# Seven products in the first layer from the third chunk on, its squares on ScalarE, three pieces of MLP work kept back

## The chip, the cores and the metric

The kernel runs on one core of a Trainium2 chip. TensorE multiplies matrices into PSUM, VectorE (DVE in the profile), ScalarE (ACT) and GpSimd (POOL) do the elementwise work, and SyncE (SP) and GpSimd issue DMA transfers. Each engine works through its own instructions in the order in which they were written and waits on semaphores for the others. The metric is the device time of the whole program in microseconds; lower is better.

## What is computed

```python
# attention: q, k, v are (8, 8, 576, 64), float32
scores = (1.0 / np.sqrt(64)) * np.matmul(q, k.transpose(0, 1, 3, 2))
thresh = np.max(scores, axis=-1, keepdims=True) - tau
scores = np.where(scores >= thresh, scores, -1000000000.0)
scores = scores - np.max(scores, axis=-1, keepdims=True)
attn = np.exp(scores)
attn = attn / (np.sum(attn, axis=-1, keepdims=True) + 1e-09)
attn_out = np.matmul(attn, v)
# bridge: (B, H, S, D) -> x of (4608, 512)
x = attn_out.transpose(0, 2, 1, 3).reshape(4608, 512)
# MLP: w_in is (512, 2048), w_out is (2048, 512)
h = x @ w_in
r = np.maximum(h, 0.0)
g = r * r
out = g @ w_out
```

## The kernel before

**Steps of attention.** Two heads (a pair) are worked on together. A step `s` takes one block of 128 query rows of one pair: scores on TensorE (line 249), their maxima on VectorE (L271), exponentials on ScalarE (L284 to L287), threshold and row sum on VectorE (L299 to L302), division on GpSimd (L307 and L309). The weights are then turned, in the first 35 steps by TensorE (L341), from step 35 on (`first_dma`) by VectorE in blocks of 32 (L381) and by DMAs (L393, L398), and multiplied with v (`mix`, L443); the result is copied into the ring of tokens `xT` (L426 to L437). There are 148 steps. The program's last pass, at step 151 (`END`), holds all that is left.

**Chunks of the MLP.** The 4608 tokens make 18 chunks of 256. A chunk's MLP work is queued when its last token is there: chunk 0 at step 10, chunk 1 at step 21, chunks 2 and 3 at step 43, then two or three at a time at steps 61, 79, 97, 115, 133 and 151. Chunk 0 (`PLAIN = 1`) is computed plainly: 16 pieces of the first layer (`mlp_in`, L491) and 16 of the second (`mlp_out`, L663). All later chunks use the seven products of a 2 x 2 block scheme (Strassen's, in Winograd's form) in both layers: 14 `unit` pieces of the first layer (seven products, two halves, L595) and 14 halves of products of the second (`product`, L698). Each piece is a group of TensorE matmuls.

**What the seven products need.** In the first layer they need differences of tokens, T1 to T4 (L568), and sums of weights (`factor_sum`, L536), made per chunk on VectorE or GpSimd, and one difference, S3, that replaces a block of `w_in` in place (`in_place`, L514). A product lands in a PSUM bank; ScalarE copies it into g (L615, L620, L624) or VectorE adds it (L607), then comes Relu on ScalarE (L603) and the square on GpSimd (L604). In the second layer they need four differences of `w_out`, made once in 16 parts (`some_sums`, L651), and differences of g (`square_half`, L481 and L482, and L718, L722).

**Order.** The order on each engine is that of the Python code. The loop over steps writes the attention instructions and calls `fill` four times per step, which takes pieces from the queue `waiting` by a planned rate (`rate`): each piece counts 1.76 us, and the rate is the smallest of "work at hand by then, divided by steps until then" over the coming arrivals and the end. A piece is also gated by how many blocks of weights have been loaded and rounded; the pieces of chunk 1 and later ask for one more than there are, which `state["usable"]` grants from step 38 on. `ask` queues sums of VectorE, `some_later` issues them one at a time between other work, and `need` issues at once what a unit is about to read. What follows a piece (copies, adds, squares) is returned as a list and written one piece later (`after`).

**Before step 43.** From step 35 on, `early_work` gives VectorE two operations per step: the four in-place differences S3 (L514), then the weight sums of chunk 1's products "6" and "5". Chunk 1 keeps its own places for sums (`home`), since g is empty then.

Of the kernel before, what the change touches and what calls it, by code (L numbers as in the profile page):

```python
# [19 lines left out]
def kernel(  # L20
# [10 lines left out]
    nc = tc.nc  # L31
# [11 lines left out]
    TCH = 2 * P  # L43
    NCH = n_tokens // TCH
    HF, HD = NFT // 2, d_model // 2
    PLAIN = 1
    SCALE = 0.125
    assert (H % 2, D, REST, NBLK, d_model) == (0, 64, 64, 4, H * D)
    assert n_tokens == B * S and n_tokens % TCH == 0 and SCALE * SCALE * D == 1.0
# [434 lines left out]
    def mlp_in(j, x):  # L484

        f, at = FORDER[x], j * TCH % RING
        if x % 2 == 0:
            used["h"] = take("mm", (6, 7))
        h = used["h"].rearrange("p (f n) -> p f n", f=2)
        for c in range(NMC):  # L490
            nc.tensor.matmul(h[:, x % 2, :], w_in_sb[:, c, f * P:(f + 1) * P], xT[:, c, at:at + TCH],  # L491
                             start=(c == 0), stop=(c == NMC - 1))
        if x == NFT - 1:
            read_to["x"] = (j + 1) * TCH
        if x % 2 == 0:
            return []

        def square():
            to = g[:, f - 1:f + 1, :]
            nc.scalar.activation(out=to, in_=h, func=AF.Relu)  # L500
            nc.gpsimd.tensor_tensor(out=to, in0=to, in1=to, op=ALU.mult)
        return [square]

    def block_of(name, q, c):
# [5 lines left out]
    def in_place():  # L510

        def one(q, c):
            to = w_in_sb[:, c, DH + q * WP:DH + (q + 1) * WP]
            nc.vector.tensor_tensor(out=to, in0=w_in_sb[:, c, q * WP:(q + 1) * WP], in1=to, op=ALU.subtract)  # L514
        return [lambda q=q, c=c: one(q, c) for q in range(2) for c in range(2)]

    def halves_of(t, lo):
        return [t[:, lo + x:lo + x + 2, :].rearrange("p f n -> p (f n)") for x in (0, 2)]
# [2 lines left out]
    low, high = ([x[:, lo:lo + HF // 2, :].rearrange("p f n -> p (f n)") for x in gsum] for lo in (0, HF // 2))  # L521

    def home(j, p, q):

        if j == PLAIN and q == 0:
            return {"6": low, "5": high, "3": gb}[p]
# [32 lines left out]
    def some_later(count=1):  # L559

        for _ in range(min(count, len(later))):
            j, p, *rest = later.popleft()
            if p[0] != "T":
                factor_sum(j, p, *rest)
                continue
            x11, x12, x21, x22 = tokens(j)
            to, a, b = {"T1": (T1, x12, x11), "T2": (T2, x22, T1), "T3": (x12, x22, x12), "T4": (T4, x21, T2)}[p]
            nc.vector.tensor_tensor(out=to, in0=a, in1=b, op=ALU.subtract)  # L568

    def need(*what):  # L570
        for x in what:
            assert x in asked
            while x in later:
                some_later()

    def unit(j, p, q):

        if (p, q) == ("1", 0):
            ask((j, "T1"), (j, "T2"), (j, "T3"))
            if j == PLAIN:  # L580
                ask((j, "3", 0, 0), (j, "3", 0, 1))
        if j == PLAIN:
            some_sums(1)
        if p in "5674":
            need((j, {"5": "T1", "6": "T2", "7": "T3", "4": "T4"}[p]))
        if (p, q) in (("3", 0), ("6", 1), ("5", 1), ("3", 1)):
            need((j, p, q, 0), (j, p, q, 1))
        x11, T3, x21, x22 = tokens(j)
        part = {"1": x11, "2": x21, "3": x22, "5": T1, "6": T2, "7": T3, "4": T4}[p]
        if p in "125":  # L590
            used[p, q] = keep_bank((p, q))
        to = used[{"6": "1", "7": "1", "4": "1", "3": "5"}.get(p, p), q].rearrange("p (f n) -> p f n", f=4)
        for f in range(4):
            for c in range(2):
                nc.tensor.matmul(to[:, f, :], factor(j, p, q, c)[:, f * P:(f + 1) * P], part[:, c, :],  # L595
                                 start=(p in "125" and f == 0 and c == 0), stop=(p in "234" and f == 3 and c == 1),
                                 skip_group_check=True)
        if (p, q) == UNITS[1][0]:
            read_to["x"] = (j + 1) * TCH
        g11, g12, g21, g22 = (g[:, lo + 4 * q:lo + 4 * q + 4, h * P:(h + 1) * P] for lo in (0, HF) for h in range(2))  # L600

        def square(to, src=None):
            nc.scalar.activation(out=to, in_=to if src is None else src, func=AF.Relu)  # L603
            nc.gpsimd.tensor_tensor(out=to, in0=to, in1=to, op=ALU.mult)  # L604

        def add(x):
            nc.vector.tensor_tensor(out=x, in0=to, in1=x, op=ALU.add)  # L607
            return [lambda: square(x)]

        def then():  # L610
            more = []
            if p == "1":
                if q:
                    need((j, "3", 0, 0), (j, "3", 0, 1))
                nc.scalar.copy(g11, to)  # L615
                ask((j, "T4"))
            elif p == "2":
                more = add(g11)
            elif p == "6":
                nc.scalar.copy(g12, to)  # L620
                if q:
                    ask((j, "3", 1, 0), (j, "3", 1, 1))
            elif p == "5":
                nc.scalar.copy(g22, to)  # L624
                if not q:
                    if j == PLAIN:
                        ask(*((j, x, 1, c) for x in "6" for c in range(2)))
# [54 lines left out]
    def product(j, x, half):  # L682
# [23 lines left out]
        def then():  # L706
# [12 lines left out]
            elif p == "6":  # L719
                tt(out=p1s, in0=to, in1=p1s, op=add)  # L720
                nc.gpsimd.tensor_tensor(out=c12, in0=p5s, in1=p1s, op=add)
                halves(lambda f: tt(out=gsum[1][:, f, :], in0=g1[:, f, 0:P], in1=gsum[1][:, f, :], op=sub))  # L722
                for c in range(2):
                    factor_sum(j + 1, "6", 0, c, nc.gpsimd)
            elif p == "7":
# [30 lines left out]
    def by_dma(n):  # L756

        return n >= 3 * HP - 1
# [25 lines left out]
            j += 1  # L784
    PIECE_US = 1.76
    VALUES_US = 4.8
    waiting = deque()
    state = {"us": 0.0, "left": 0.0, "step": 0, "free": False, "rounded": 0, "usable": 0, "then": [], "last": []}

# [20 lines left out]
    def rate(s):  # L810


        if s < out_from:
            return PIECE_US * sum(x[2] == 0 for x in waiting) / (out_from - s)
        have = PIECE_US * len(waiting) - state["left"]
        best = 1e9
        at = s
        for e in sorted(chunk_at) + [END]:
            if e > s:
                have += sum(VALUES_US for x in range(at, e) if x in mixes and by_dma(mixes[x][0]))  # L820
                at = e
# [13 lines left out]
    def piece():  # L835
        _, fn, *what = waiting.popleft()
        state["left"] -= PIECE_US
        if fn is mlp_out or what[0] < PLAIN and what[1] == 0 or what == [PLAIN, "1", 0]:
            after()
        then = fn(*what)  # L840
        after()
# [29 lines left out]
    early_work = deque()  # L871

    def end_rounding(p):
        round_weights(p, 4)
# [54 lines left out]
    rounded_by = [0]  # L929
    for s in range(END + 1):  # L930
        state["step"] = s
        state["usable"] = rounded_by[-1] + (s > first_dma + 2)
        if s == 2:
            startup.close()
            bpsum = ctx.enter_context(tc.tile_pool(name="bpsum", bufs=1, space=bass.MemoryType.PSUM))
            bank.update((x, bpsum.tile([P, 512], FP32, tag=f"bank{x}", name=f"bank{x}")) for x in range(4, 8))
        rounded_by.append(state["rounded"])
        if s == first_dma:
            assert read_to["x"] == PLAIN * TCH
            work = in_place() + [lambda p=p, c=c: factor_sum(PLAIN, p, 0, c) for p in ("6", "5") for c in range(2)]  # L940
# [57 lines left out]
        if on:  # L998
# [78 lines left out]
```

## Time and profile before

| | |
|---|---|
| median of 3 runs | 1403.05 us (1402.34 to 1405.98) |
| the profiled execution | 1405.17 us, of which the span is 1403.4 us |
| mean granted TensorE clock | 0.984 |
| busy in the span | TensorE 1327.7 us (95%), VectorE 1039.1 (74%), GpSimd 1011.6 (72%), ScalarE 503.9 (36%) |
| exponentials, L287 | 269 at 731 ns |
| division, L309 | 269 at 915 ns |
| Relu of the first layer, L603 | 102 at 630 ns from SBUF, 34 at 596 ns from PSUM |
| square, L604 | 136 at 1072 ns |
| addition of a product, L607 | 102 at 679 ns |

Times of the profile come from one execution. Busy time of TensorE is modelled from starts, since matmuls are pipelined, so it shows where the engine has work in hand rather than how well it is used; a float32 matmul appears as two records. A line such as `A <- B: t, n, m` in a list of waits says that A waited for B for t us in n places, m us at the longest. In a group's line the count and the busy time come first, then the mean, then the idle time before it and what ended that. In a cut of the span by windows each engine has its busy time and the number of its instructions, and then come the granted clock, the share of the DMA engines and GB/s.

### The profile page before, as it was taken

How to read it: one execution, taken by the hardware profiler on the slowest of the kernel's cores; microseconds unless marked ns; L12 is line 12 of the kernel's file. 1: busy time of each engine (PE TensorE's matmuls, PEld its weight loads, DVE VectorE, ACT ScalarE, POOL GpSimd, SP SyncE). 2: the span in 40 equal slices, each digit the busy share in tenths (PEclk: the TensorE clock that was granted, in tenths of full speed). 3: DMA queues.
4: the chain of work that ended last, by engine and by line, in shares of the span. 5: the costliest groups of instructions: out<-in, count | busy, mean ns of one | idle time of the engine just before them, and what ended most of it. 6: DMA issues, size and time to landing. Idle time of an engine off the chain costs nothing.

```text
span 1403.4 us, 26562 instructions
## 1 busy us (share of the span) xinstructions
PE 1327.7 (95%) x9208; PEld 1075.2 (77%) x9208; DVE 1039.1 (74%) x2180; ACT 503.9 (36%) x1187; POOL 1011.6 (72%) x1273
## 2 busy tenths in 40 slices
PE   6899997799999999889999999999999999999998
PEld 5676565678787878668787878788878777889998
DVE  6877777778897978796887878888887787823341
ACT  4777673223333333323232323232423232411211
POOL 3689774478878879786777879879787877634433
PEclk8999998799999999999999999999999999999999
DMA  7765432225655536353544545455555445330000
GB/s 152 158 150 141 119 81 59 52 46 117 100 118 99 121 74 120 71 111 75 106 90 89 110 89 111 101 94 120 99 106 101 83 92 99 80 71 1 16 16 15
DMA packets 407893, 128.19 MB, mean 91 GB/s; under 512 B 390832, under 2 KB 396752, under 8 KB 407760
## 3 DMA queue, kind: packets, MB, share of 16 engines
q1 hardware_dynamic: 385632, 95.10, 36.3%
q0 software_dynamic: 19824, 31.11, 8.5%
q8 instruction: 74, 1.21, 0.4%
q10 hardware_dynamic: 2304, 0.29, 0.2%
q14 instruction: 59, 0.48, 0.1%
HBM read 50.59 MB, written 9.44 MB: 43 GB/s over the span
## 4 chain that ended last, share of the span: by engine, by line
PE 73%; DVE 8%; POOL 7%; ACT 3%; issue 3%; SPq 3%; DMA 2%; ACTq 0%; DVEq 0%; POOLq 0%
PE bank L698 24%; PE bank L595 24%; PE s L249 10%; PE bank L443 10%; SPq L393 2%; PE bank L663 2%; DVE st L271 2%; PE bank L341 2%; POOL g L536 1%; POOL w L309 1%; DVE w L299 1%; DVE turned L381 1%; PE bank L491 1%; ACT w L287 1%; DMA wT<-turned 1%
## 5 line engine op out<-in xcount | busy, mean ns | idle before, releaser
L271 DVE TENSOR_REDUCE st<-s 128x1 f32<-128x576 f32 x286 | 203.5, 749 | 124.1 <-PE s L249 123.5
L299 DVE SCALAR_TENSOR_TENSOR w<-s,st,w 128x576 f32<-128x576 f32 x269 | 208.9, 813 | 68.0 <-ACT w L287 67.6
L309 POOL TENSOR_SCALAR w<-w,st 128x576 f32<-128x576 f32 x269 | 243.7, 915 | 21.5 <-DVE st L302 13.1
L698 PE MATMUL bank<-wo,gsum 128*128 128x256 f32 x1088 | 245.8, 382 | 0.9 <-DVE gsum L722 0.9
L604 POOL TENSOR_TENSOR g<-g 128x512 f32<-128x512 f32 x136 | 145.3, 1072 | 126.9 <-ACT g L603 119.0
L698 PEld LDWEIGHTS bank<-wo,gsum 128*128 128x128 f32 x1088 | 204.0, 190 | 40.9 <-issue 11.2
L595 PE MATMUL bank<-xT,w_in_sb 128*128 128x128 f32 x1632 | 200.8, 280 | 4.6 <-ACT xT L426 2.5
L595 PEld LDWEIGHTS bank<-xT,w_in_sb 128*128 128x128 f32 x1632 | 193.0, 195 | 15.7 <-issue 7.7
L698 PE MATMUL bank<-wo,g 128*128 128x256 f32 x816 | 187.7, 383 | 2.3 <-POOL g L604 2.1
L249 PE MATMUL s<-kT,qT 64*128 64x288 f32 x1016 | 169.6, 433 | 17.8 <-DVE w L299 13.4
L287 ACT ACTIVATE w<-s,st 128x576 f32<-128x576 f32 x269 | 183.2, 731 | 0.4 <-ACT st L285 0.2
L381 DVE STREAM_TRANSPOSE turned<-w 128x512 f32<-128x512 f32 (+2 forms) x388 | 169.3, 490 | 15.6 <-DMA wT<-turned 8.9
L284 ACT ACTIVATE st<-st 128x2 f32<-128x2 f32 (+1 forms) x148 | 30.3, 205 | 417.7 <-DVE st L271 417.1
L443 PE MATMUL bank<-wT,vs 128*64 128x128 f32 (+7 forms) x1700 | 168.2, 356 | 8.2 <-ACT wT L342 3.9
L698 PEld LDWEIGHTS bank<-wo,g 128*128 128x128 f32 x816 | 150.7, 190 | 31.5 <-issue 6.8
L443 PEld LDWEIGHTS bank<-wT,vs 128*64 128x64 f32 (+1 forms) x1700 | 95.5, 136 | 79.9 <-issue 25.2
L249 PEld LDWEIGHTS s<-kT,qT 64*128 64x128 f32 x1016 | 96.8, 188 | 65.7 <-issue 39.4
L307 POOL TENSOR_SCALAR st<-st 128x2 f32<-128x2 f32 (+1 forms) x148 | 36.1, 244 | 131.3 <-DVE w L299 122.6
L595 PE MATMUL bank<-t,g 128*128 128x128 f32 x784 | 103.0, 288 | 19.7 <-DVE g L536 11.6
L595 PEld LDWEIGHTS bank<-t,g 128*128 128x128 f32 x784 | 96.1, 200 | 27.2 <-DVE g L536 12.8
L607 DVE TENSOR_TENSOR g<-bank,g 128x512 f32<-128x512 f32 x102 | 69.3, 679 | 54.8 <-PE bank L595 54.8
L603 ACT ACTIVATE g<-g 128x512 f32<-128x512 f32 x102 | 63.6, 630 | 111.5 <-DVE g L607 111.5
(113 smaller groups left out, 1907.8 us busy)
## 6 DMA issues: line engine op xcount, KB each, us to landing
wT<-turned SPq DMA_DIRECT2D x800, 72.0 KB, 2.4
wo<-in_moe_w_in_dram SPq DMA_DIRECT2D x16, 512.0 KB, 4.9
wo<-in_moe_w_out_dram SPq DMA_DIRECT2D x16, 512.0 KB, 3.6
out_dram<-osb POOLq DMA_DIRECT2D x32, 256.0 KB, 2.8
ql<-in_q_dram POOLq DMA_DIRECT2D x96, 72.0 KB, 3.0
wT<-turned SPq DMA_DIRECT2D x192, 36.0 KB, 2.3
kl<-in_k_dram POOLq DMA_DIRECT2D x88, 72.0 KB, 3.4
vs<-in_v_dram POOLq DMA_DIRECT2D x48, 128.0 KB, 3.1
```

The source lines that it names most:

```text
L249: nc.tensor.matmul(sc[u][to, half, 0:HALF], lhsT, keys[rows, half * HALF:(half + 1) * HALF], start=True, stop=True)
L271: nc.vector.tensor_reduce(out=mx[:, u:u + 1], in_=sc[u][:, :, 0:HALF], axis=AX.XY, op=ALU.max)
L287: nc.scalar.activation(out=w[:, u, :].rearrange("p (h k) -> p h k", h=2), in_=sc[u][:, :, 0:HALF], func=AF.Exp, bias=bias[:, u:u + 1], sca ...
L299: nc.vector.scalar_tensor_tensor(out=wu, in0=sc[u][:, :, 0:HALF], scalar=thr[:, u:u + 1], in1=wu, op0=ALU.is_ge, op1=ALU.mult, accum_out=s ...
L309: nc.gpsimd.tensor_scalar(out=w[:, u, :], in0=w[:, u, :], scalar1=z[:, u:u + 1], scalar2=rcp[:, u:u + 1], op0=ALU.add, op1=ALU.mult)
L381: nc.vector.transpose(wb[:, at:at + k1 - k0, i % 2, :], w[:, u, k0 * 32:k1 * 32].rearrange("p (k q) -> p k q", q=32))
L443: nc.tensor.matmul(ps[u * D:(u + 1) * D, :], vs[n % 2][rows, u * (NBLK + 1) + c, :], wT[rows, NBLK if c == NBLK else u * (NBLK + 1) + c, a ...
L595: nc.tensor.matmul(to[:, f, :], factor(j, p, q, c)[:, f * P:(f + 1) * P], part[:, c, :], start=(p in "125" and f == 0 and c == 0), stop=(p ...
L603: nc.scalar.activation(out=to, in_=to if src is None else src, func=AF.Relu)
L604: nc.gpsimd.tensor_tensor(out=to, in0=to, in1=to, op=ALU.mult)
L607: nc.vector.tensor_tensor(out=x, in0=to, in1=x, op=ALU.add)
L698: nc.tensor.matmul(to, left[:, f, :], wo[:, slot, f, :], start=(f == 0), stop=(f == HF - 1))
```

## The change

Chunk 1 gets the plain first layer too, with the squares on GpSimd and `square_half` after them, and the seven products in the second (`SEVEN = 2`). Its gate asks for the loaded weights only. The first layer of later chunks squares on ScalarE. The in-place S3 is asked for at the end of chunk 1's first layer. The 16 differences of `w_out` follow chunk 1's first-layer pieces. `rate` leaves three pieces (`RESERVE`) at each arrival but the end. `early_work` and the special places of chunk 1's sums are gone; `need` is renamed `demand`.

```diff
-    PLAIN = 1
+    PLAIN, SEVEN = 1, 2
...
         if x % 2 == 0:
-            used["h"] = take("mm", (6, 7))
+            used["h"] = take("mm", (6, 7)) if j < PLAIN else next_bank()
...
         if x == NFT - 1:
             read_to["x"] = (j + 1) * TCH
-        if x % 2 == 0:
-            return []
-
-        def square():
-            to = g[:, f - 1:f + 1, :]
-            nc.scalar.activation(out=to, in_=h, func=AF.Relu)
-            nc.gpsimd.tensor_tensor(out=to, in0=to, in1=to, op=ALU.mult)
-        return [square]
+            if j == SEVEN - 1:
+                ask(*((j, "S3", q, c) for q in range(2) for c in range(2)))
+        posts = [lambda: some_sums(1)] if j >= PLAIN else []
+        if x % 2:
+            def square():
+                to = g[:, f - 1:f + 1, :]
+                nc.scalar.activation(out=to, in_=h, func=AF.Relu)
+                nc.gpsimd.tensor_tensor(out=to, in0=to, in1=to, op=ALU.mult)
+                if j >= PLAIN and x % 8 == 7:
+                    square_half(x // 8 * (HF // 2))
+            posts.append(square)
+        return posts
...
             j, p, *rest = later.popleft()
+            if p == "S3":
+                q, c = rest
+                to = block_of("S3", q, c)
+                nc.vector.tensor_tensor(out=to, in0=block_of("A11", q, c), in1=to, op=ALU.subtract)
+                continue
...
         def square(to, src=None):
             nc.scalar.activation(out=to, in_=to if src is None else src, func=AF.Relu)
-            nc.gpsimd.tensor_tensor(out=to, in0=to, in1=to, op=ALU.mult)
+            nc.scalar.activation(out=to, in_=to, func=AF.Square)
...
                 halves(lambda f: tt(out=gsum[1][:, f, :], in0=g1[:, f, 0:P], in1=gsum[1][:, f, :], op=sub))
+                if j == SEVEN - 1:
+                    demand(*((j, "S3", x, c) for x in range(2) for c in range(2)))
                 for c in range(2):
                     factor_sum(j + 1, "6", 0, c, nc.gpsimd)
...
+    RESERVE = 3 * PIECE_US
...
+        todo = [((x // 4 + 1) * NMC, mlp_in, j, x) for x in range(NFT)]
         if j < PLAIN:
-            todo = [((x // 4 + 1) * NMC, mlp_in, j, x) for x in range(NFT)]
             todo += [(n_in + min(f + 1 + f // (NFT - 2), NFT), mlp_out, j, f) for f in range(NFT)]
         else:
-            second = [(n_pieces + 1, product, j, x, half) for x in range(len(PRODUCTS)) for half in range(2)]
-            todo, rest = ([(n_pieces + 1, unit, j, *x) for x in part] for part in UNITS)
+            second = [(n_pieces, product, j, x, half) for x in range(len(PRODUCTS)) for half in range(2)]
+            if j < SEVEN:
+                return todo + second
+            todo, rest = ([(n_pieces, unit, j, *x) for x in part] for part in UNITS)
             todo += second[0:2] + rest + second[2:]
...
-                best = min(best, have / (e - s))
+                best = min(best, (have - (RESERVE if e < END else 0)) / (e - s))
...
-        return best - (VALUES_US if s in mixes and by_dma(mixes[s][0]) else 0.0)
+        return max(best, 0.0) - (VALUES_US if s in mixes and by_dma(mixes[s][0]) else 0.0)
...
-        state["usable"] = rounded_by[-1] + (s > first_dma + 2)
+        state["usable"] = rounded_by[-1]
...
-        if s == first_dma:
-            assert read_to["x"] == PLAIN * TCH
-            work = in_place() + [lambda p=p, c=c: factor_sum(PLAIN, p, 0, c) for p in ("6", "5") for c in range(2)]
-            early_work.extend([work[x], work[x + 1]] for x in range(0, len(work), 2))
...
-            for fn in early_work.popleft() if early_work else ():
-                fn()
```

More of the change, by code (lines that the diff above doesn't have):

```diff
@@ L508, in block_of @@
         return w_in_sb[:, 2 * col + c, at:at + WP]
[L510 to L515, printed above, removed]
     def halves_of(t, lo):
@@ L523, in home @@
     def home(j, p, q):
-        if j == PLAIN and q == 0:
-            return {"6": low, "5": high, "3": gb}[p]
         return {("6", 0): ga, ("5", 0): gb, ("3", 0): low, ("6", 1): high, ("5", 1): gb, ("3", 1): high}[p, q]
@@ L568, in some_later, with demand @@
             nc.vector.tensor_tensor(out=to, in0=a, in1=b, op=ALU.subtract)
-    def need(*what):
+    def demand(*what):
         for x in what:
@@ L579, in unit @@
             ask((j, "T1"), (j, "T2"), (j, "T3"))
[L580 to L583, printed above, removed]
         if p in "5674":
-            need((j, {"5": "T1", "6": "T2", "7": "T3", "4": "T4"}[p]))
+            demand((j, {"5": "T1", "6": "T2", "7": "T3", "4": "T4"}[p]))
         if (p, q) in (("3", 0), ("6", 1), ("5", 1), ("3", 1)):
-            need((j, p, q, 0), (j, p, q, 1))
+            demand((j, p, q, 0), (j, p, q, 1))
         x11, T3, x21, x22 = tokens(j)
@@ L613, in then @@
                 if q:
-                    need((j, "3", 0, 0), (j, "3", 0, 1))
+                    demand((j, "3", 0, 0), (j, "3", 0, 1))
                 nc.scalar.copy(g11, to)
@@ L625, in then @@
                 if not q:
-                    if j == PLAIN:
-                        ask(*((j, x, 1, c) for x in "6" for c in range(2)))
                     ask((j, "5", 1, 0), (j, "5", 1, 1))
@@ L837, in piece @@
         state["left"] -= PIECE_US
-        if fn is mlp_out or what[0] < PLAIN and what[1] == 0 or what == [PLAIN, "1", 0]:
+        if fn is mlp_out or what[0] <= PLAIN and what[1] == 0:
             after()
@@ L869 @@
     assert out_from <= first_dma
-    early_work = deque()
     def end_rounding(p):
```

## The prediction

> **What bounds the kernel now.** I read the page's chain first, then its slices, then cut the span at the steps around the edit, then asked for TensorE's waits on either side.
>
> ```profile
> PE 73%; DVE 8%; POOL 7%; ACT 3%; issue 3%; SPq 3%; DMA 2%; ACTq 0%; DVEq 0%; POOLq 0%
> PE   6899997799999999889999999999999999999998
> PEclk8999998799999999999999999999999999999999
> ```
>
> The chain lies on TensorE for 73% of the span. In the slices TensorE is full except at the start and in slices 7 and 8 (210 to 280 us), where its granted clock sags too. Next, that stretch cut at the first score matmul of steps 35 to 42 (columns: TensorE, weight loads, VectorE, ScalarE, GpSimd, clock, DMA share, GB/s).
>
> ```profile
> 212.20:219.40 7.20, 7.20 (x45) 4.10 (x45) 4.66 (x11) 3.40 (x9) 3.33 (x5) 1.00 0.26 44
> 219.40:224.20 4.80, 3.15 (x41) 2.45 (x41) 2.39 (x5) 3.64 (x10) 1.88 (x3) 1.00 0.28 109
> 224.20:231.20 7.00, 2.85 (x29) 1.79 (x29) 5.84 (x14) 2.14 (x8) 2.62 (x3) 1.00 0.00 0
> 231.20:253.00 21.80, 17.29 (x88) 15.19 (x89) 15.68 (x33) 3.93 (x8) 9.62 (x11) 0.69 0.45 82
> 253.00:269.00 16.00, 10.81 (x74) 9.51 (x73) 11.50 (x23) 2.87 (x6) 3.53 (x4) 0.89 0.15 28
> 269.00:284.80 15.80, 11.71 (x74) 10.23 (x73) 12.88 (x20) 4.47 (x9) 10.98 (x12) 0.78 0.42 76
> 284.80:293.20 8.40, 8.40 (x59) 7.22 (x58) 6.57 (x15) 3.03 (x7) 3.63 (x5) 1.00 0.11 19
> 293.20:301.60 8.40, 8.40 (x43) 6.61 (x42) 6.38 (x13) 1.93 (x5) 8.07 (x12) 1.00 0.18 40
> ```
>
> Steps 36 and 37 have almost no MLP work, step 38 has five units of chunk 1 at once, and steps 38 to 40 take 16 to 22 us each where 41 and 42, with four pieces each, take 8.4. The eight steps last 89.4 us. TensorE's own waits here, then those between 301 and 1217 us, then busy times after 301.6 us:
>
> ```profile
> PE bank L595 <- DVE gsum L536: 6.9, 3, 3.3
> PE bank L595 <- DVE g L536: 5.6, 3, 3.3
> PE s L249 <- DVE w L299: 5.4, 2, 4.1
> ```
> ```profile
> PE bank L595 <- DVE g L536: 7.5, 4, 2.9
> PE bank L595 <- DVE t L568: 5.5, 1, 5.5
> PE bank L698 <- POOL g L604: 2.1, 2, 1.8
> ```
> ```profile
> 301.60:1216.80 915.20, 887.28 (x6137) 721.08 (x6136) 749.86 (x1595) 302.33 (x710) 741.10 (x972) 0.99 0.52 99
> 1216.80:1403.40 186.60, 182.95 (x1225) 166.05 (x1224) 65.32 (x108) 33.34 (x66) 74.26 (x70) 1.00 0.11 25
> ```
>
> Units wait for VectorE's sums of weights (L536) and token differences (L568). From 301.6 us on TensorE idles 27.9 us (915.2 - 887.28), and in the tail nothing of weight: there it sets the time alone. So the kernel is TensorE work plus 19.6 us of early holes (89.4 - 69.8 busy), the clock lost beside them, and 28 us of scattered waits.
>
> **Price of a piece.** Start to start in the timeline of a stretch without waits:
>
> ```profile
> 481.46 3.74 PE L595 MATMUL bank<-xT,w_in_sb 128*128 128x128 f32 x32
> 438.29 7.17 PE L698 MATMUL bank<-wo,g 128*128 128x256 f32 x32
> 84.52 1.89 PE L491 MATMUL bank<-xT,w_in_sb 128*128 128x256 f32 x8
> ```
>
> Two units 3.6 us (the next group starts at 485.03), four product halves 7.1 (445.39), one plain first-layer piece 1.8 (86.34). Every piece is 1.8 us.
>
> **Part 1, chunk 1's first layer plain, started earlier.** It becomes 16 pieces instead of 14 units: 2 x 1.8 = 3.6 us more TensorE work. The gate on steps past 37 goes with it. By the two instruction lists, pieces of chunk 1 per step from 35 to 42 are
>
> ```
> before  0 0 0 5 4 4 4 4   (21 of 28, 7 left)
> after   2 4 3 4 3 4 3 4   (27 of 30, 3 left)
> ```
>
> Each new step is the larger of TensorE's sum and VectorE's chain. TensorE: step 35 was full, 7.2 + 2 x 1.8 = 10.8; step 36, 3.15 + 7.2 = 10.4, taken as 10.0 because 3.15 holds modelled ends; step 38, scores 1.2 + 7.2 = 8.4; step 40, eight score matmuls 2.2 + 7.2 = 9.4; step 41, 1.2 + 5.4 = 6.6; step 42 is today's row, 8.4. VectorE: two reduces (1.4), two threshold operations (1.6), small ones (0.5), transposes (1.5, some steps 0.8 more), and in steps 36 to 40 two to four of the 16 sums of the second weights (L651, 0.68 each alone), 7.4 to 8.0 in all; it also waits for the exponentials, 1.1 us (the wait of L299 in step 37), partly filled by a sum. That gives 9.2 in step 37, 9.0 in 38, 7.8 in 39, where TensorE needs less. Sum: 10.8 + 10.0 + 9.2 + 9.0 + 7.8 + 9.4 + 6.6 + 8.4 = 71.2, which is 18.2 less than 89.4. Four pieces fewer are left for the full stage behind: 4 x 1.8 = 7.2. **Part 1 is worth 25 us**, the two extra pieces included.
>
> Off VectorE in these steps go chunk 1's differences, its weight sums and its six additions (L607, 0.69 each). What stays is moved: the four in-place S3 subtractions (L514, 0.68 each) leave steps 35 and 36 for steps 40 and 41, behind the last first-layer matmul that reads the old block; the wait is at most that piece, 1.8 us, and behind it on VectorE stand the next step's reduces, for which ScalarE and then TensorE's next scores wait. Product "6" of chunk 1 asks for all four, long issued by then, so nothing. Chunk 1's squares are ScalarE then GpSimd (0.6 + 1.05), eight each; the last four rows of g are needed by product "4", 3.6 us after "1" begins: covered. Until step 37 the first layer has only banks 6 and 7: a bank is wanted again after 3.6 us and Relu takes 0.6, but ScalarE's queue has the exponentials in it. Lower end no wait; upper end one exponential wait (VectorE's reduce late by 6.1 us in step 38) in each of two steps, 12 us. I take zero, because Relu follows the exponentials by less than a pair in the new order, and keep 12 for a rival.
>
> **Part 2, the square on ScalarE.** 128 GpSimd multiplications go, 128 Squares come.
>
> ```profile
> L604 POOL TENSOR_TENSOR g<-g 128x512 f32<-128x512 f32 x136 | 145.3, 1072 | 126.9 <-ACT g L603 119.0
> L603 ACT ACTIVATE g<-g 128x512 f32<-128x512 f32 x102 | 63.6, 630 | 111.5 <-DVE g L607 111.5
> ```
>
> GpSimd loses 128 x 1.07 = 137 us and the waits for Relu in front of them, behind which the divisions (L309) and the load issues (L193) stand in its queue. Square is not in the trace; the nearest row is Relu on the same shape, 0.63, so ScalarE gains 128 x 0.63 = 81 us (504 to 585, 42%). In the new ScalarE order Square follows its Relu, behind the step's exponentials, into idle time (111.5 us before these Relus alone). Without that cover all 81 us lie before the next exponentials. A rule speaks against this part: the Trainium skill, "ScalarE: Activation LUTs" (What ACT_TABLE_LOAD costs), prices each switch to another set of functions at about 2.66 us. If Square were not in the set of Exp, up to two switches per Square make 128 x 5.3 = 680 us. The trace has one load of 1.28 us for Exp, Relu and Copy together, and the changed instruction list has one too; I take zero.
>
> Two effects on TensorE. The two waits on L604 go: 2.1. And VectorE gets faster: between 301 and 1217 us its sums of two SBUF tensors average 0.99 (L722), 1.05 and 1.09 (two groups of L536), where the median of L722 is 0.68; 26 of each, with the milder groups, make 33 us of excess, while L607, with one input in PSUM, stays at 0.68. "SBUF — State Buffer" of the same skill (SBUF: two separate sides) says that VectorE with two SBUF inputs and GpSimd lock one port pair against each other and that ScalarE has its own. By rows alone I could not credit the move with anything; by the rule, L604's share of GpSimd's tensor time there (109.7 of 436 us) gives 8 us. Half falls where VectorE is what units wait for: 4. With the 2.1: **6 us**.
>
> **Part 3, three pieces held back.** At step 79 three chunks arrive with nothing left, and the first units wait for their differences, queued behind four weight sums: the 5.5 us of L568. With three pieces over, product "3" of the old chunk comes while the new one is already there and asks for T1 to T3 first. That hole goes (next late are the weight sums, L536); the clock around it, 0.79, costs some 2 more. **7 us.** The pieces held are done one chunk later, and at the end none is held: the tail (182 us) has the same order, so nothing there. The wait for xT right behind its copy (2.5 in four places) may go or stay: nothing taken.
>
> **Sum.** 25 + 6 + 7 = 38 us. The profiled execution took 1405.2 (span 1403.4 and 1.8 around it), so 1367 for it; the median of the runs is 2.1 lower, 1403.05: **1365**.
>
> **Rivals.** (a) The later waits only move. U-dense steps leave VectorE 95% busy before and after, and the new split of units over steps makes new holes: only part 1 stays, 1378. For it: the density is unchanged (four units in the worst step). Against: the 5.5 is one queue order, which changes. (b) Steps 36 to 40 stay bound by VectorE and the two banks, 12 us of part 1 lost: 1377; with (a) 1390. (c) Most of the 28 us goes, and VectorE's relief is worth its whole 8: 25 + 28 = 53, 1350. (d) Slower: ScalarE's queue. A Square in front of an exponential delays threshold and next scores by 0.63; it decides once the mean delay that reaches TensorE passes 38 / 128 = 0.30 us; at the full 81 the time is 1446. Against: ScalarE waits 384 us for VectorE's maxima after 301 us. (e) The change does nothing: the planner could leave the pieces where they were; the lists exclude it.
>
> **How the numbers follow.** Forecast 0.47 (own range 1358 to 1372), (a) 0.22, (b) 0.12, (c) 0.12, (d) 0.05, all parts cancelling 0.02. A measurement of this kernel tells 0.3% (4.2 us) from no change. Leaving out (d), the cancelling case and the outer ends of (b) and (c) gives 1348 to 1384. Faster 0.93, same 0.02, slower 0.05.
>
> **What would show it.** Steps 35 to 42 in about 71 us at a clock near 1.00, none over 11; no GpSimd square outside chunks 0 and 1; Square at 0.6; L536's and L722's means nearer 0.68; no wait over 3 us on a token difference; TensorE idle under 18 us from there to the tail. I am wrong if steps 36 to 40 run at 11 us or more, if ScalarE's exponentials start later after the reduce than today, or if new waits on weight sums replace the old.

## The result, and the profile after

| | before | changed |
|---|---|---|
| median | 1403.69 us (4 runs, 1402.34 to 1405.98) | 1389.79 us (4 runs, 1386.62 to 1390.00) |
| ratio to before | | 0.989, 95% interval 0.987 to 0.991 |
| span of the profiled execution | 1403.4 us | 1384.8 us |
| mean granted TensorE clock | 0.984 | 0.991 |

The change is 1.1% faster. I had forecast 1365 us, 1348 to 1384, so the direction is right, the time lies outside the range, and the gain is a little over a third of the forecast one. The changed kernel's profiled execution is shorter than its median, so the spans differ by 18.6 us where the medians differ by 13.9. What follows is read from the spans; the 4.7 us between the two differences vary from run to run, and no trace shows them.

The page of the changed kernel: the chain that ended last, by engine, and the rows of slices.

```profile
PE 72%; DVE 10%; SPq 6%; ACT 4%; issue 3%; DMA 3%; POOL 2%; ACTq 0%; DVEq 0%; POOLq 0%
PE   6899999999999999989999999999999999999998
PEclk8999999999999999999999999999999999999999
```

The hole at slices 7 and 8 is gone, and the granted clock is full there. SyncE's queue went from 3% to 6% of the chain. Steps 35 to 42 of the changed kernel, cut as before at their first score matmul (same columns):

```profile
212.20:224.30 12.10, 11.03 (x63) 7.15 (x63) 4.12 (x11) 4.44 (x11) 4.47 (x7) 1.00 0.27 70
224.30:234.50 10.20, 10.20 (x73) 8.30 (x72) 8.31 (x15) 4.25 (x12) 4.27 (x5) 1.00 0.00 0
234.50:242.00 7.50, 7.50 (x55) 5.93 (x54) 5.60 (x13) 2.95 (x7) 2.79 (x4) 1.00 0.01 2
242.00:250.20 8.20, 8.20 (x42) 6.89 (x42) 8.13 (x14) 2.63 (x6) 5.50 (x6) 1.00 0.65 112
250.20:256.40 6.20, 6.20 (x30) 5.09 (x28) 6.13 (x15) 1.51 (x4) 6.08 (x8) 1.00 0.65 126
256.40:267.00 10.60, 8.81 (x49) 6.70 (x49) 10.52 (x19) 2.90 (x7) 7.28 (x8) 1.00 0.39 72
267.00:273.60 6.60, 6.59 (x34) 5.27 (x34) 5.44 (x13) 1.66 (x4) 3.77 (x8) 1.00 0.85 132
273.60:281.80 8.20, 8.20 (x41) 6.64 (x40) 6.03 (x15) 1.92 (x5) 6.57 (x11) 1.00 0.36 67
```

They last 69.6 us; 89.4 before, 71.2 foretold. So at step 43 the changed kernel is 19.8 us ahead. It does not get further. The rest of the span in three stretches (steps 43 to 79, 80 to 146, the tail), first the kernel before, then the changed one:

```profile
301.60:621.10 319.50, 307.64 (x2105) 247.15 (x2104) 266.07 (x559) 103.88 (x248) 259.17 (x346) 0.99 0.52 99
621.10:1216.80 595.70, 579.63 (x4033) 473.93 (x4032) 483.79 (x1037) 198.45 (x462) 481.93 (x627) 0.99 0.51 99
```
```profile
281.80:592.70 310.90, 299.16 (x2041) 239.79 (x2040) 247.87 (x551) 121.44 (x279) 219.37 (x310) 0.99 0.55 102
592.70:1197.90 605.20, 587.52 (x4066) 481.04 (x4066) 487.73 (x1046) 241.36 (x534) 406.89 (x559) 0.99 0.50 97
1197.90:1384.80 186.90, 183.15 (x1225) 166.09 (x1224) 68.89 (x107) 49.70 (x92) 47.51 (x43) 1.00 0.11 25
```

Steps 43 to 79 take 8.6 us less, steps 80 to 146 take 9.5 more, the tail is the same. By counting pieces, TensorE has four pieces and the three held ones less in the first stretch (7 x 1.8 = 12.6) and the three more in the second (5.4). So the time that isn't pieces rose by about 4 us in each, where I had taken 13 off. TensorE's idle time from step 43 to the tail, span minus busy, went from 27.9 to 29.4 us instead of falling under 18. The rest of the rise lies in busy time as the profile models it and is not taken apart here.

TensorE's waits in steps 43 to 79, first the longest of the kernel before, then those of the changed one:

```profile
PE bank L595 <- DVE g L536: 5.2, 2, 2.9
PE bank L595 <- ACT g L620: 2.1, 1, 2.1
```
```profile
PE bank L443 <- issue: 4.5, 4, 1.4
PE s L249 <- DVE w L299: 3.8, 3, 1.5
PE bank L590 <- DVE gsum L530: 1.7, 2, 1.5
PE bank L590 <- DVE t L567: 0.9, 1, 0.9
```

The waits on a token difference (L567) are down to 0.9. The two of before are gone too, but now the mix matmuls (L443) stop four times in the middle, and the next scores (L249) wait for thresholds that came late.

The 5.5 us wait of step 80 is gone, but the stretch around it is not shorter. Steps 80 to 84, 18 pieces in both kernels, before and changed, and then TensorE's waits there in the changed kernel:

```profile
621.10:673.10 52.00, 46.00 (x330) 38.81 (x329) 38.58 (x81) 17.80 (x39) 39.99 (x53) 0.93 0.41 87
592.70:646.60 53.90, 47.09 (x340) 39.22 (x340) 39.40 (x90) 21.12 (x46) 31.20 (x45) 0.97 0.40 83
```
```profile
PE bank L590 <- DVE gsum L530: 3.5, 2, 2.1
PE bank L590 <- DVE g L530: 1.7, 1, 1.7
```

Step 80 itself fell from 16.3 to 10.9 us, and steps 81 to 84 grew by as much and more: there the units wait for weight sums (L530) instead.

The square on ScalarE takes what Relu takes, and VectorE's sums got cheaper. In order: Square, and the four groups of VectorE's sums with two SBUF inputs that had the largest means before (0.78 to 1.09 us), in steps 43 to 146 of the changed kernel.

```profile
L599 ACT ACTIVATE g<-g x128: 629/630/638, 305.9 to 1362.3; 128x512 f32<-128x512 f32 x128
```
```profile
L530 DVE TENSOR_TENSOR gsum<-w_in_sb,gsum 128x512 f32<-128x512 f32 x26 | 25.5, 997 | 0.0
L715 DVE TENSOR_TENSOR gsum<-g,gsum 128x512 f32<-128x512 f32 x26 | 22.0, 885 | 0.0
L530 DVE TENSOR_TENSOR gsum<-w_in_sb,g 128x512 f32<-128x512 f32 x26 | 20.0, 791 | 0.0
L530 DVE TENSOR_TENSOR g<-gsum,w_in_sb 128x512 f32<-128x512 f32 x26 | 19.2, 748 | 0.0
```

Before, the same groups of 26 took 28.0, 24.7, 19.6 and 26.9 us. That is 99.2 then and 86.7 now, 12.5 us less of VectorE. Not all of it is the square's: the experiments below separate it.

### The profile page after: what moved, and what is told of

The parts are those of the page before. It is cut to its first block, busy times and chain, and to the rows that moved or that the text cites. A ratio compares the mean times of both kernels' runs of the same rounds, so it can differ in the third digit from the quotient of the medians.

```text
span 1384.8 us, 26329 instructions
## 1 busy us (share of the span) xinstructions
PE 1324.4 (96%) x9112; PEld 1069.9 (77%) x9112; DVE 1016.6 (73%) x2158; ACT 577.5 (42%) x1309; POOL 867.0 (63%) x1145
## 4 chain that ended last, share of the span: by engine, by line
PE 72%; DVE 10%; SPq 6%; ACT 4%; issue 3%; DMA 3%; POOL 2%; ACTq 0%; DVEq 0%; POOLq 0%
PE bank L590 23%; PE bank L691 22%; PE s L249 10%; PE bank L443 9%; SPq L393 6%; PE bank L491 3%; DVE turned L381 2%; PE bank L656 2%; DVE st L271 2%; DMA wT<-turned 2%; PE bank L341 2%; DVE w L299 1%; ACT w L287 1%; ACT wT L342 1%; DVE gsum L715 1%
## 5 line engine op out<-in xcount | busy, mean ns | idle before, releaser
L309 POOL TENSOR_SCALAR w<-w,st 128x576 f32<-128x576 f32 x269 | 231.7, 870 | 27.4 <-DVE st L302 22.6
L691 PEld LDWEIGHTS bank<-wo,gsum 128*128 128x128 f32 x1088 | 204.6, 190 | 40.6 <-issue 11.1
L249 PE MATMUL s<-kT,qT 64*128 64x288 f32 x1016 | 171.6, 435 | 18.9 <-DVE w L299 12.5
L590 PE MATMUL bank<-xT,w_in_sb 128*128 128x128 f32 x1536 | 185.1, 277 | 0.0
L590 PEld LDWEIGHTS bank<-xT,w_in_sb 128*128 128x128 f32 x1536 | 178.7, 192 | 7.4 <-issue 5.3
L443 PE MATMUL bank<-wT,vs 128*64 128x128 f32 (+7 forms) x1700 | 169.2, 356 | 13.3 <-issue 4.5
L443 PEld LDWEIGHTS bank<-wT,vs 128*64 128x64 f32 (+1 forms) x1700 | 96.3, 136 | 84.4 <-issue 30.9
L249 PEld LDWEIGHTS s<-kT,qT 64*128 64x128 f32 x1016 | 98.0, 189 | 68.5 <-issue 40.7
L481 POOL TENSOR_TENSOR gsum<-g 128x512 f32<-128x512 f32 x34 | 47.8, 1407 | 90.3 <-ACT g L599 89.9
L590 PE MATMUL bank<-t,g 128*128 128x128 f32 x768 | 96.4, 280 | 7.4 <-DVE g L530 4.4
L602 DVE TENSOR_TENSOR g<-bank,g 128x512 f32<-128x512 f32 x96 | 65.3, 680 | 50.2 <-PE bank L590 48.5
L590 PEld LDWEIGHTS bank<-t,g 128*128 128x128 f32 x768 | 90.1, 193 | 15.0 <-DVE g L530 5.5
L193 POOL DMA_DIRECT2D vs<-in_v_dram x144 | 89.8, 631 | 0.0
```

What stands on the lines that cost most here:

```text
L193: (nc.gpsimd if state["step"] > first_dma + 2 else nc.sync).dma_start(out=to, in_=src)
L249: nc.tensor.matmul(sc[u][to, half, 0:HALF], lhsT, keys[rows, half * HALF:(half + 1) * HALF], start=True, stop=True)
L309: nc.gpsimd.tensor_scalar(out=w[:, u, :], in0=w[:, u, :], scalar1=z[:, u:u + 1], scalar2=rcp[:, u:u + 1], op0=ALU.add, op1=ALU.mult)
L443: nc.tensor.matmul(ps[u * D:(u + 1) * D, :], vs[n % 2][rows, u * (NBLK + 1) + c, :], wT[rows, NBLK if c == NBLK else u * (NBLK + 1) + c, a ...
L691: nc.tensor.matmul(to, left[:, f, :], wo[:, slot, f, :], start=(f == 0), stop=(f == HF - 1))
```

## The experiments

Each number below is a median with the ratio to the kernel before and its 95% interval.

**The parts one by one.** Four kernels. Nothing held back:

```diff
-    RESERVE = 3 * PIECE_US
+    RESERVE = 0 * PIECE_US
```

> The changed kernel with nothing held back (RESERVE = 0); all else as changed. Theory A (the reserve lengthens the way to the mixes: with it the first mix of each pair of visits stands behind unit pieces in steps 48, 57, 66 and 75, and only 11 pieces instead of 12 lie between it and the next mix four steps later, which then waits for the DMAs that turn the weights): those waits of mix matmuls, 8.9 us in the changed kernel between steps 43 and 146, fall to about 3, and the wait for T1 at step 80 (5.5 us and the clock) comes back; between 1380 and 1388 us, so 2 to 8 us faster than the changed kernel. Theory B (the reserve is worth its 7 us, as predicted, and the square on ScalarE eats it): 1395 to 1398 us.

Measured: 1399.07 us, 0.997 (0.996 to 0.998).

The square of the seven products back on GpSimd:

```diff
-            nc.scalar.activation(out=to, in_=to, func=AF.Square)
+            nc.gpsimd.tensor_tensor(out=to, in0=to, in1=to, op=ALU.mult)
```

> The changed kernel with the square of the first layer's seven products back on GpSimd; all else as changed. Theory A: the square on ScalarE is worth a few us in waits for GpSimd and in VectorE's faster sums, so this runs at 1392 to 1398 us. Theory B (Squares in front of exponentials delay the score chain): 1378 to 1384 us. If VectorE's relief goes to waste because the units' waits lie elsewhere: 1390 within 1.5.

Measured: 1394.35 us, 0.993 (0.991 to 0.994).

Both of these edits together, so the plain and early first layer of chunk 1 alone:

> Part 1 alone: chunk 1's first layer plain and early, squares of the seven products on GpSimd, nothing held back. By the prediction's part 1 (25 us): 1378 to 1380 us. If the parts add up as Theory A has them: the time of the kernel without reserve plus what the GpSimd square costs, 1386 to 1392 us.

Measured: 1405.65 us, 1.0014 (1.0005 to 1.0023).

The square alone, in the kernel before:

```diff
-            nc.gpsimd.tensor_tensor(out=to, in0=to, in1=to, op=ALU.mult)
+            nc.scalar.activation(out=to, in_=to, func=AF.Square)
```

> The kernel before with one line changed: the square of the seven products on ScalarE. By the prediction's part 2: 6 us faster than before, 1397 to 1398 us. If VectorE's relief is worth its whole 8 us or more: 1393 to 1396. Theory B: 1405 us or more.

Measured: 1393.03 us, 0.992 (0.991 to 0.994).

Both theories on the reserve fell with the first of these. Without it the kernel is 9 us slower, not faster. (The 8.9 us of that expectation is 7.7 in the lists of waits: 4.5 of mixes that stop in the middle, 3.2 of mixes that wait for an addition of VectorE.) And the layer that I had priced at 25 us gives nothing alone; beside the square it costs 6.0 (1393.03 to 1399.07). The trace of the kernel with the early layer alone tells why. Its steps 35 to 42 take 74.7 us, 14.7 less than before, but step 44 takes 19.6 us (8.3 before). The largest of TensorE's waits between 285 and 625 us and the place itself:

```profile
PE bank L590 <- DVE t L567: 13.2, 2, 8.3
```
```profile
306.50 0.65 DVE L530 TENSOR_TENSOR gsum<-w_in_sb,g 128x512 f32<-128x512 f32 x1
307.07 1.28 DVE L530 TENSOR_TENSOR gsum<-w_in_sb 128x512 f32<-128x512 f32 x2
308.27 0.41 DVE L567 TENSOR_TENSOR t<-xT 128x256 f32<-128x256 f32 x1
308.83 6.23 PE L590 MATMUL bank<-t,g 128*128 128x128 f32 x32 [8.32 <-DVE t L567]
```

Chunk 1 is now finished when chunks 2 and 3 arrive at step 43. The first units of chunk 2 come at once, and their token differences stand on VectorE behind a step's score work and the sums of weights: 8.3 us. The kernel before was behind with chunk 1 at that step (seven pieces left), so its differences were asked for in time. It has this wait only at step 80. So the early layer brings its own new wait, at steps 44 and 62, and the reserve is what removes it.

The square alone did on TensorE what the prediction's two terms say. From 300 to 1217 us the waits on GpSimd's squares (2.1 us before) are gone, and those on the weight sums that were 7.5 us are

```profile
PE bank L595 <- DVE g L536: 3.5, 2, 1.8
```

That is the 6 us foretold. The kernel gained 11.1 at the median (from 1404.10, the kernel before in the same series; 12.2 in the spans); 3.2 us of it lie in steps 35 to 42 (86.2 instead of 89.4), where the changed kernel has no seven products any more. VectorE's four groups took 90.7 us there, 8.5 less than before. The same edit is worth 12.0 us of VectorE with three pieces held (98.7 to 86.7) and only 1.9 with none (97.8 to 95.9), so what it saves depends on what stands beside what.

**How many pieces.** The instruction lists show that the count of held pieces moves two other things. The last request for the differences hangs on the first half of product "3", the last but one piece. And the first mix of each pair of visits, in steps 48, 57, 66 and 75, stands ahead of the step's pieces, or behind some of them while more than two PSUM banks are held. In the traces it stands behind two pieces in each of these steps with three held, and ahead of all with two or one. In the changed kernel, two held and then one:

```diff
-    RESERVE = 3 * PIECE_US
+    RESERVE = 2 * PIECE_US
```
```diff
-    RESERVE = 3 * PIECE_US
+    RESERVE = 1 * PIECE_US
```

> The changed kernel with two pieces held back instead of three. By the two instruction lists the token differences are still asked for ahead of a new chunk's units, but in steps 48, 57, 66 and 75 the mix now stands ahead of the unit pieces, and 12 instead of 11 pieces follow until the next mix. Theory A (what the changed kernel still loses lies in mixes that wait for their transfers): the mixes' own waits and the score waits behind them fall by 5 to 10 us and the time to 1379 to 1386. If the position of the mix is harmless and the waits only come from lighter steps: 1389 within 2.

> The changed kernel with one piece held back. The mixes stand as with two, but the one piece left is the second half of product 3, and it is the first half that asks for the new chunk's differences. Theory C (the reserve is worth what the first units wait for their token differences at steps 44, 62 and 80, and nothing else): as slow as with nothing held back, 1397 to 1400. If each held piece is worth its share of the 9 us: 1394 to 1397, between none and two.

Measured: two held, 1373.86 us, 0.979 (0.977 to 0.980), faster than either expectation. One held, 1398.38 us, 0.997 (0.995 to 0.998), as if nothing were held. TensorE's longest waits from 285 to 620 us (steps 43 to 80, in part to 82), with two held and then with one:

```profile
PE bank L590 <- DVE g L530: 7.2, 5, 2.4
```
```profile
PE bank L590 <- DVE t L567: 20.1, 3, 8.3
```

One piece between one and two is worth 24.5 us: it carries the request, and the three waits of up to 8.3 us, at steps 44, 62 and 80, appear without it. One piece between two and three costs 15.9 us at the median and 13.2 in the spans (1371.6 and 1384.8). The steps of the second mix and the ones behind them (52 and 53, 61 and 62, 70 and 71, 79 and 80), which have the same number of pieces in both, take 81.2 us with three and 68.0 with two: 13.2 us, as much as the spans differ by. What the other steps win and lose evens out.

The way between two mixes, in the changed kernel and with two held. SyncE's queue and the mix matmuls, steps 66 to 70; first the changed kernel:

```profile
480.47 4.79 PE L443 MATMUL bank<-wT,vs 128*64 128x320 f32 x40
507.70 0.76 PE L443 MATMUL bank<-wT,vs 128*64 128x320 f32 x4
509.60 2.83 PE L443 MATMUL bank<-wT,vs 128*64 128x256 f32 x21 [1.15 <-issue]
```
```profile
485.28 22.12 SPq L393 DMA_DIRECT2D wT<-turned  x32
```
```profile
509.57 1.50 DVE L381 STREAM_TRANSPOSE turned<-w 128x576 f32<-128x576 f32 x3 [4.56 <-DMA wT<-turned]
```

Two held:

```profile
477.19 4.79 PE L443 MATMUL bank<-wT,vs 128*64 128x320 f32 x40
508.17 4.79 PE L443 MATMUL bank<-wT,vs 128*64 128x320 f32 x40
```
```profile
482.00 21.89 SPq L393 DMA_DIRECT2D wT<-turned  x32
```

The turned weights have one place. The next ones can come when a mix has read them, and SyncE then issues 32 transfers one after the other, 22.1 us, the last landing 2.4 us later (the median landing of this form). So here a mix can't run sooner than some 24 us after the end of the one before. With three held the first mix ends at 485.26 and the second is reached at 507.70, 22.4 later, with 10 pieces between (the expectations have 11); it does four matmul records and stops until 509.60. VectorE stands still 4.6 us for the same transfers and goes on at 509.57, so the next scores are late too. (The profile names no releaser for the stop of the mix; that it waits for the transfers is read from these times.) With two held the mix ends at 481.98, the transfers take as long (21.9 us), but 12 pieces stand between, the way is 26.2 us, and the second mix runs in one. The ways of the other three pairs are the same to 0.1 us, 22.4 with a stop each and 26.2 without. No run moves the first mix alone: the edit also changes which pieces stand in these steps.

**The other way to an early request.** Nothing held back, but the differences go to the head of VectorE's list when a chunk comes and no unit is waiting:

```diff
     def add_chunk(j):
+        if j >= SEVEN and not any(x[1] is unit for x in waiting):
+            for x in ("T3", "T2", "T1"):
+                if (j, x) not in asked:
+                    asked.add((j, x))
+                    later.appendleft((j, x))
         waiting.extend(pieces_of(j))
```

> Nothing held back, but a new chunk's three token differences are put at the head of VectorE's queue when the chunk arrives. Theory C: the waits on token differences (13 us at steps 44 to 62 in the kernel with part 1 alone) fall to about 3, and the time from 1399 to 1384 to 1390, without any reserve. If the wait is for VectorE as such, busy with the scores' work, and not for the order in its queue: 1396 to 1400.

Measured: 1390.89 us, 0.991 (0.990 to 0.992). The request alone is worth 8.2 us, about as much as three held pieces (9.3); step 44 falls from 20.0 to 8.6 us. So the wait was for the order of VectorE's list, not for VectorE as such. The time is just past the expected range; the waits for one kind of weight sums (g, L530) are 6.8 us there and 4.2 with nothing held, which may be why.

**Two queues for the transfers.** In the changed kernel, eight of the 32 transfers go to ScalarE's queue:

```diff
-                    nc.sync.dma_start(out=to[:, :, at:at + 64], in_=wb[rows, j::4, :, :].rearrange("p c u q -> p c (u q)"))
+                    queue = nc.scalar if pair == 1 and j % 2 else nc.sync
+                    queue.dma_start(out=to[:, :, at:at + 64], in_=wb[rows, j::4, :, :].rearrange("p c u q -> p c (u q)"))
```

> The changed kernel (three held back), with half of the transfers of the second pair of blocks issued from ScalarE's queue instead of SyncE's. Theory A, in the form that the transfers' issue on one queue (0.7 us each, 16 to a pair) sets when the second mix can run: the waits of mixes at steps 52, 61, 70 and 79 shrink and the time falls by 3 to 8 us, to 1382 to 1387. If the wait is for the first mix to set the turned weights' place free, or if ScalarE loses by the issues what the mixes win: 1388 to 1395.

Measured: 1472.79 us, 1.049 (1.048 to 1.051), outside both expectations. This does not test the queue. ScalarE's own order now stops where a transfer has to wait (lines behind the edit have numbers one higher in this kernel):

```profile
ACT g L599 <- DMA wT<-turned: 53.8, 6, 10.7
ACT st L284 <- DMA wT<-turned: 44.0, 4, 13.1
ACT g L611 <- DMA wT<-turned: 41.0, 5, 10.3
```

That the 32 issues one after the other set the refill's time rests on the sum above and on the run with two held, not on a run with a faster queue. Why one issue takes some 0.69 us stays open.

**What the early layer is worth beside the rest.** The kernel before with the square on ScalarE and with a reserve of two, then of three:

```diff
-            nc.gpsimd.tensor_tensor(out=to, in0=to, in1=to, op=ALU.mult)
+            nc.scalar.activation(out=to, in_=to, func=AF.Square)
...
+    RESERVE = 2 * PIECE_US
...
-                best = min(best, have / (e - s))
+                best = min(best, (have - (RESERVE if e < END else 0)) / (e - s))
...
-        return best - (VALUES_US if s in mixes and by_dma(mixes[s][0]) else 0.0)
+        return max(best, 0.0) - (VALUES_US if s in mixes and by_dma(mixes[s][0]) else 0.0)
```

> The kernel before with the square on ScalarE and two pieces held back, so without the plain and early first layer of chunk 1; against the changed kernel with two held back (1373.9) it gives what that layer is worth once the waits on token differences and the late mixes are out of the way. If its 25 us then come through whole: 1397 to 1400, which would need the reserve to cost something here. If the reserve takes only the hole at step 80 (5.5 us and the clock) off the kernel with the square alone (1393.0): 1384 to 1388, and the layer is worth 10 to 14. If the reserve does nothing without it: 1393, and the layer is worth 19.

> The same with three pieces held back. By the instruction list no mix of steps 48 to 79 stands behind units except the one of step 79's batch, so Theory A expects no loss against two: within 3 us of it. If three pieces are bad as such, as they are in the changed kernel: 10 us or more above it.

Measured: 1398.34 us, 0.997 (0.995 to 0.998), and 1402.60 us, 0.999 (0.998 to 1.000). Without the early layer the reserve costs 5 and 10 us against the square alone. It takes away the 5.5 us of step 80 and brings others: with two held, step 59 takes 14.4 us instead of 8.3, where a product waits 2.9 us for g from ScalarE, and step 82 17.4 instead of 8.4, where units wait 4.5 us for weight sums. The third piece costs 4.3 there, between the two expectations.

**The square beside two held.** Two edits in the changed kernel:

```diff
-    RESERVE = 3 * PIECE_US
+    RESERVE = 2 * PIECE_US
...
-            nc.scalar.activation(out=to, in_=to, func=AF.Square)
+            nc.gpsimd.tensor_tensor(out=to, in0=to, in1=to, op=ALU.mult)
```

> Two held back with the square of the seven products on GpSimd. If the square is worth what it is beside three held back (4.6 us): 1378 to 1380. If it is worth what it is alone (11 us): 1383 to 1387.

Measured: 1377.02 us, 0.981 (0.980 to 0.982), just under the lower expectation. The square is worth 3.2 us here, 4.6 with three held, 6.6 with none, 11.1 alone in the kernel before. It is worth less the faster the kernel is otherwise. That fewer waits are left for it to shorten is a likely reason, not a shown one.

**Five held.** In the changed kernel:

```diff
-    RESERVE = 3 * PIECE_US
+    RESERVE = 5 * PIECE_US
```

> The changed kernel with five pieces held back. By the instruction list the mixes of steps 48, 57, 66 and 75 stand ahead of all but two units, as with two held back, and the token differences are asked for well ahead. Theory A (three is bad because of where it puts the mixes): within 6 us of the kernel with two, 1368 to 1380. If every piece held beyond two costs something of itself: 1390 or more.

Measured: 1385.40 us, 0.986 (0.985 to 0.988), between the expectations. The stopped mixes are absent, as expected, and the eight steps around the second mixes take 70.0 us, close to the 68.0 with two held. But steps 43 to 79 as a whole, with as many pieces, take 313.0 us (299.3 with two, 310.9 with three). Among the waits are scores waiting for a transposed q (L229), at steps 45, 54, 63 and 72:

```profile
PE s L249 <- DVE qT L229: 5.2, 4, 2.5
```

Further on, steps 106 and 145 take 14.5 and 13.4 us; a mix waits 2.4 us for an addition of VectorE (L602) in the one, a unit 2.9 for a token difference in the other. What sets these was not followed up. So the mixes' place is not all that a count of held pieces moves; two is the best of 0, 1, 2, 3 and 5 (four was not run), and I have no rule that says so beforehand.

## Why the prediction was wrong

*Steps 35 to 42, 18.2 us.* Right in sum: 19.8, with the clock at 1.00. Single steps were off by up to 1.7 both ways (step 37 took 7.5, not 9.2; step 40 took 10.6, not 9.4), so part of the hit is luck. Step 35 took 12.1 where none was to be over 11: a piece of the first layer waited 1.1 us for one of the two banks, which I had taken as nothing.

*"Four pieces fewer are left for the full stage behind", 7.2 us.* The work did go: the counts of pieces are seven less and three more. What was wrong is to price it as part 1's own. I took the stage as full because it was full before. With chunk 1 done in time and nothing held back the queue is empty at step 43, and the first units of chunk 2 wait for differences nobody has asked for. Alone, the layer moved the time by +0.1%. Its 25 us come out only beside the two other parts and with two pieces held: 1398.34 to 1373.86 is 24.5. With three held it is 12.8 (1402.60 to 1389.79).

*The square, 6 us.* Right in kind: one table load as before, 0.63 us each. The exponentials' chain starts 0.03 us after VectorE's reduce in both kernels, so rival (d) did not occur. In the kernel before, the two terms measured what I had said, and VectorE's relief was 8.5 us where I had worked out 8; the edit was worth 11.1 there and 4.6 in the changed kernel. I had added the parts as if each kept its worth beside the others.

*Three held back, 7 us.* This is the step that failed, twice. The wait of step 80 went as described, but waits for weight sums came behind it, which I had named as "next late" and priced at nothing: steps 80 to 84 take 53.9 us where they took 52.0. And "the pieces held are done one chunk later" has no cost in my sum. Holding pieces shifts every later piece against the steps. I priced the hole that closes and not what the shift moves: the first mix of each pair of visits went behind two pieces, the second was then reached before its transfers had landed, and the eight steps involved lost 13.2 us against two held. The room for this could be read in the trace of before, in SyncE's queue and the two mixes around it:

```profile
502.83 4.79 PE L443 MATMUL bank<-wT,vs 128*64 128x320 f32 x40
507.64 21.50 SPq L393 DMA_DIRECT2D wT<-turned  x32
531.78 2.43 PE L443 MATMUL bank<-wT,vs 128*64 128x320 f32 x18
```

The first mix ended at 507.6 and the next came at 531.8. 21.5 and 2.4 to land make 23.9, so the kernel before had 0.3 us to spare here, with 11 pieces between. Its other ways of this kind were 28.0 us or more.

In the sum: 38 were forecast, the spans show 18.6. The first eight steps gave 1.6 more than said; the 13 of the two other parts did not appear, since the time from step 43 to the end that isn't pieces rose by about 8 instead of falling. With two held, steps 43 to 79 and 80 to 146 are

```profile
287.30:586.50 299.20, 294.31 (x2041) 234.03 (x2040) 250.94 (x554) 122.78 (x279) 221.94 (x312) 1.00 0.58 106
586.50:1184.60 598.10, 585.79 (x4057) 481.18 (x4056) 484.05 (x1038) 241.36 (x532) 405.39 (x558) 0.99 0.51 99
```

That is 897.3 us, and TensorE idles 17.2 of them; the sum had asked for 915.2 - 7.2 - 13 = 895.0 (893.2 with the one piece less that this kernel has left at step 43) and under 18. The median of that kernel, 1373.86, lies in the range. So 15.9 of the 24.8 us by which the forecast missed are the third piece. That the sum then nearly fits is in part luck: with two held step 82 takes 16.4 us, and the square is worth 3.2 instead of 6.

Of the rivals, (a), "the later waits only move", is what happened. At steps 80 to 84 they moved to the weight sums, and "new waits on weight sums replace the old" was among my signs of being wrong. The larger part, a transfer queue, no rival named; (a)'s 1378 was too low, because waits did not only move but grew. (b) did not occur, but for the one wait of 1.1 us, and (d) not at all. I had (a) and (b) together at 1390 and left that outside the range; that this is the measured time is chance. I held no case in which the parts hurt each other.

## What to carry to other kernels

Where a written order interleaves two streams of work, an edit that shifts one by a few pieces is not free because the work is the same. Ask for each resource with one place (here the turned weights) how long its refill takes and how much room the order leaves it; a row of a DMA queue between two uses gives both. And when a stage becomes lighter, look at what was made early only because it was late: a backlog hides the time in which the next chunk's operands are made. Try a reserve's size one piece at a time: 0, 1, 2, 3 and 5 gave 1399, 1398, 1374, 1390 and 1385 us.

## What the runs showed of the hardware

In the kernel with the early layer alone, a TensorE wait cost more than its length. Behind the 8.3 us wait of step 44 (300.5 to 308.8 us), two units took 6.2 us where they take 3.7 in a stretch without waits. The granted clock was 0.50 from within the wait until the units were nearly done, and 0.74 over the whole step:

```profile
295.40:315.00 19.60, 11.28 (x74) 10.46 (x73) 9.88 (x22) 3.35 (x7) 10.82 (x18) 0.74 0.67 135
303.70:313.90 10.20, 5.07 (x24) 5.10 (x25) 4.09 (x9) 0.59 (x1) 2.89 (x5) 0.50 0.63 119
```

Transfers issued from ScalarE's queue stopped ScalarE for up to 13.1 us where they had to wait, and that kernel was 83 us slower than the changed one. And 32 transfers of 72 KB from SyncE's queue took 21.5 to 22.1 us to issue, while one lands 2.4 us (median) after its issue (0.67 to 0.69 us for one issue, worked out from these).
